# Threshold attention and a gated feed-forward part on one core: the kernel lays its own steps on the engines, and q, k and v come laid out for it

## The chip, the core and the metric

The kernel runs on one core of one Trainium2 chip. Five engines work there, each through its own instructions in order: PE (TensorE, matmuls and transposes into PSUM; its weight loads are listed as PEld), DVE (VectorE), ACT (ScalarE), POOL (GpSimd) and SP (SyncE, which here issues all DMAs). They wait for one another by semaphores. The metric is the device time of one execution in microseconds; lower is better.

## The reference

Eight batches, eight heads, 576 tokens, 64 channels a head. The first part is attention whose probabilities below a threshold are cut off; the second is a feed-forward part that mixes each token with the one before it.

```python
scores = scale * np.matmul(q, k.transpose(0, 1, 3, 2))
thresh = np.max(scores, axis=-1, keepdims=True) - tau
scores = np.where(scores >= thresh, scores, -1000000000.0)
attn = np.exp(scores - np.max(scores, axis=-1, keepdims=True))
attn = attn / (np.sum(attn, axis=-1, keepdims=True) + 1e-09)
x = np.matmul(attn, v)          # heads side by side: (8, 576, 512)
...
xk = mu_k * x + (1.0 - mu_k) * x_prev
xr = mu_r * x + (1.0 - mu_r) * x_prev
k = np.maximum(xk @ w_k, 0.0)   # w_k 512 x 1024
v = k * k @ w_v                 # w_v 1024 x 512
r = 1.0 / (1.0 + np.exp(-(xr @ w_r)))
return r * v
```

The weights come as float64 words, everything else as float32.

## The kernel before

**Precision.** Most products are made from split operands: a number is written as an upper part (a copy into a shorter float format, `fp32r`) and a lower part (what is left). A product then takes three matmuls, upper by upper, upper by lower and lower by upper. Making the two parts costs a copy on ACT and a subtraction on DVE or POOL.

**Attention.** A *job* is a batch and a pair of heads, 32 in all. Each has nine *query tiles* of 128 rows: four for each head, and one tile, called T, with the last 64 queries of both heads. A *slot* is a tile, 288 in all. In `prep_steps` a job's q and k are loaded as they lie, turned on PE (L189), copied and split by ACT, DVE and POOL into `hi` and `lo`, and `stack` copies these by DMA (L238 to L241) into stationaries `st` that hold a head's upper and lower part on top of each other, so that two matmuls of 128 rows do the three products. A tile then goes through `scores` (PE, L326), `row_max` (DVE, L338), `threshold` and `expo` (ACT, L342, L346), `mask` (DVE, L351), `denom` and `inverse` (DVE, L355, L358), `norm` (POOL, L361), `turn_p` (PE, five transposes, L368), `p_hi` (ACT, L393), `p_lo` (DVE, two instructions, L403), and, for a group of two tiles and a part of T, `attend` (PE, nine matmuls, L439) and `attend_out` (ACT L447, DVE L449 and L456), which writes x transposed into `xT` (first 512 tokens of a batch, two buffers) and `xE` (last 64).

The first jobs are made otherwise: job 0 multiplies scores in plain float32 (L308), and jobs 0 to 4 multiply probabilities by values in plain float32 (L412), which leaves out the split.

**Feed-forward part.** A *chunk* is 256 tokens; there are 18, two for each batch and two for the last 64 tokens of four batches each. `mix_steps` makes and splits xk and xr (POOL L485, L504, L510; ACT L497, L507). PE multiplies by w_k (tile h), w_r (z) and w_v (vps), all on L525; ACT takes the positive part (L551), DVE squares it (L554), ACT and POOL split it (L557, L558); the gate is on L586 and L590, its product with vps on DVE (L616), the store on L619. The weights are cut to float32 and split in 20 pieces by `weight_steps`, one every two slots from slot 4 on.

**Order.** The order is written by hand in `slot(n)`, which issues the steps of slot n together with those of the four tiles before it. Feed-forward matmuls are given out by a credit: a slot counts for 3.325 us of PE, what attention needs is taken off, and the rest is filled with steps of about 1.3 us; ten steps are kept in hand while chunks are still to come.

```python
TSLOT, TSTEP, KEEP, N0 = 3.325, 1.3, 10, 36
PLAIN, WHOLE = 5, 1
...
state["credit"] += TSLOT - tensor_time()
...
while state["credit"] > 0 and micro(keep):
    state["credit"] -= TSTEP
```

PSUM holds two buffers of scores, one of turned probabilities (`pt`) and two that all other products share. The first chunk can start when all four jobs of batch 0 are done, behind slot 36.

Of the kernel before, what the change touches and what calls it, by code (L numbers as in the profile page):

```python
# [8 lines left out]
F32 = mybir.dt.float32  # L9
# [6 lines left out]
# float32 readings of the upper words of the doubles 2**-127 and just under 2**128  # L16
W_MIN = 2.0 ** (0x38 * 2 - 127)
W_MAX = 2.0 ** (0x8F - 127) * (1 + 0x6FFFFF / 2.0**23)


@with_exitstack
def tile_threshold_attention_then_rwkv_ffn(
    ctx: ExitStack,
    tc: tile.TileContext,
    q: bass.AP,
    k: bass.AP,
    v: bass.AP,
    tau: bass.AP,
    mu_k: bass.AP,
    mu_r: bass.AP,  # L30
# [5 lines left out]
    nc = tc.nc  # L36
    V, A, G, PE, SY = nc.vector, nc.scalar, nc.gpsimd, nc.tensor, nc.sync

    B, H, S, D = q.shape
    DM, DF = w_k.shape  # L40
    P = 128
    NPAIR = H // 2
# [4 lines left out]
    NC4 = SM // P  # L47
    HS = S // 2
    KT = S
    KM = S + ST  # L50
# [4 lines left out]
    assert 2 * D == P and ST == D and NPAIR == NCT and B % NTB == 0  # L55
# [9 lines left out]
    wts = ctx.enter_context(tc.tile_pool(name="wts", bufs=1))  # L65
    p1 = ctx.enter_context(tc.tile_pool(name="p1", bufs=1))
    p2 = ctx.enter_context(tc.tile_pool(name="p2", bufs=2))
    p3 = ctx.enter_context(tc.tile_pool(name="p3", bufs=3))
    ps_s = ctx.enter_context(tc.tile_pool(name="ps_s", bufs=2, space=bass.MemoryType.PSUM))
    ps_t = ctx.enter_context(tc.tile_pool(name="ps_t", bufs=1, space=bass.MemoryType.PSUM))  # L70
    ps_w = ctx.enter_context(tc.tile_pool(name="ps_w", bufs=2, space=bass.MemoryType.PSUM))
    ctx.enter_context(tc.manual_schedule(engines={A.engine}))

    ident = const.tile([P, P], F32, name="ident")
    make_identity(nc, ident)
# [3 lines left out]
    tau_s = const.tile([P, 1], F32, name="tau_s")  # L79
    SY.dma_start(tau_s, tau.rearrange("(o t) -> o t", o=1).broadcast_to([P, 1]))  # L80
    ntau = const.tile([P, 1], F32, name="ntau")
    V.tensor_scalar(ntau, tau_s, 0.0, -1.0, op0=ALU.max, op1=ALU.mult)
    qscale = const.tile([P, 1], F32, name="qscale")
    V.tensor_scalar(qscale, tau_s, 0.0, 0.125, op0=ALU.is_ge, op1=ALU.mult)

    mu_sb = const.tile([P, 2, NCT], F32, name="mu_sb")
# [3 lines left out]
    xT = []  # L90
    for j in range(2):
        t = const.tile([P, NCT, SM + 1], F32, name=f"xT{j}")
        V.memset(t[:, :, 0:1], 0.0)
        xT.append(t)
    xE = const.tile([P, NCT, NE, ST + 1], F32, name="xE")

    vraw = const.tile([P, 2, 5 * D], F32, name="vraw")

    # stationaries of the scores' tile that holds both heads' last 64 queries
    bd = const.tile([P, 4, P], FR, name="bd")  # L100
    V.memset(bd.bitcast(F32), 0.0)

    # The weights come as float64 words.  Each is cut to float32 (saturating, with what
# [78 lines left out]
    def prep_steps(job):  # L182
# [48 lines left out]
        def stack(h):  # L231
            if job["whole"]:
                return
# [750 lines left out]
```

## Time and profile before

| | |
|---|---|
| Median of two runs | 1150.68 us (1149.67 to 1151.69) |
| Profiled execution | 1151.2 us from the first to the last instruction, 22514 instructions |
| Bytes moved by DMA | 105.61 MB in 125027 packets, 93681 of them under 512 B |
| Granted TensorE clock, mean | 0.995 |

The page's second part shows the span in 40 equal slices of 28.8 us; each digit is the busy share in tenths, 9 being 90% or more:

```profile
PE   6999989999999999989999999999999999999998
DVE  3899998888989898988989898989898989895222
ACT  3787877778687878768777878787878787876442
POOL 1465677465656465645747575656565656564672
DMA  5777334433344344433334444423344444300000
```

The first slices hold loading, weights and attention alone; the last three and a half hold the feed-forward part alone, in which only PE is full. A busy digit of PE says little by itself, because matmuls overlap one another and a row of waiting ones looks like a row of dense ones; the start times of neighbouring matmuls tell more. The chain of work that ended last goes over PE for 65% of the span, over DVE for 18% and over ACT for 10%.

### The profile page before, as it was taken

What the parts mean: (1) busy time and instruction counts of PE and PEld (TensorE: products, weight loads), DVE (VectorE), ACT (ScalarE), POOL (GpSimd) and SP (SyncE); (2) the same over time, 40 slices, a digit from 0 to 9 for tenths busy, and PEclk for the clock granted to TensorE, in tenths of its full rate; (3) what the DMA queues carried; (4) which work ended last, traced back from release to release, by engine and by line L of the source; (5) the groups of instructions that cost most, each with busy time, mean ns of one, the idle gap of its engine ahead of it and who ended that gap; (6) DMA issues with size and microseconds to landing.
All of it is one profiled execution on the core that took longest, in us unless ns stands there. A gap on an engine that the chain in (4) does not pass through costs nothing.

```text
span 1151.2 us, 22514 instructions
## 1 busy us (share of the span) xinstructions
PE 1104.4 (96%) x7454; PEld 999.1 (87%) x7454; DVE 961.3 (84%) x2399; ACT 846.0 (73%) x1775; POOL 673.3 (58%) x860
## 2 busy tenths in 40 slices
PE   6999989999999999989999999999999999999998
PEld 4887878898989898988989898989898989898997
DVE  3899998888989898988989898989898989895222
ACT  3787877778687878768777878787878787876442
POOL 1465677465656465645747575656565656564672
PEclk9999999999999999999999999999999999999999
DMA  5777334433344344433334444423344444300000
GB/s 131 184 205 204 83 85 93 113 85 74 70 95 105 84 112 95 112 88 71 83 83 104 92 104 104 99 68 87 79 102 94 104 98 99 76 29 13 25 20 18
DMA packets 125027, 105.61 MB, mean 92 GB/s; under 512 B 93681, under 2 KB 101873, under 8 KB 124913
## 3 DMA queue, kind: packets, MB, share of 16 engines
q1 hardware_dynamic: 124912, 104.18, 38.8%
q8 instruction: 60, 0.98, 0.3%
q14 instruction: 55, 0.44, 0.1%
HBM read 39.85 MB, written 9.44 MB: 43 GB/s over the span
## 4 chain that ended last, share of the span: by engine, by line
PE 65%; DVE 18%; ACT 10%; issue 4%; SPq 1%; DMA 1%; POOL 1%; DVEq 0%; ACTq 0%; POOLq 0%
PE h L525 12%; PE vps L525 12%; PE pt L368 10%; PE s L326 9%; PE o L439 9%; PE z L525 8%; DVE p L351 4%; DVE sm L338 3%; DVE plo L403 2%; ACT phi L393 2%; ACT p L346 2%; DVE r L554 2%; PE o L412 1%; DVE phi L403 1%; DVE xT L137 1%
## 5 line engine op out<-in xcount | busy, mean ns | idle before, releaser
L361 POOL TENSOR_SCALAR p<-p,sm 128x576 f32<-128x576 f32 x288 | 222.6, 773 | 255.2 <-DVE sm L358 187.4
L393 ACT ACTIVATE phi<-pt 128x640 fp32r<-128x640 f32 (+1 forms) x270 | 172.4, 649 | 111.3 <-PE pt L368 110.6
L351 DVE SCALAR_TENSOR_TENSOR p<-s,sm,p 128x576 f32<-128x576 f32 x288 | 233.7, 811 | 23.4 <-ACT p L346 19.1
L338 DVE TENSOR_REDUCE sm<-s 128x1 f32<-128x576 f32 x288 | 215.9, 750 | 21.2 <-PE s L308 10.3
L525 PE MATMUL h<-xk,wk 128*128 128x256 f32 x1728 | 231.8, 285 | 1.0 <-ACT r L551 0.3
L525 PE MATMUL vps<-wv,k 128*128 128x512 f32 x864 | 227.2, 399 | 2.0 <-DVE sg L616 1.8
L368 PE MATMUL pt<-ident,p 128*128 128x128 f32 x1440 | 210.4, 276 | 18.6 <-DVE phi L403 8.9
L525 PEld LDWEIGHTS h<-xk,wk 128*128 128x128 f32 x1728 | 216.0, 191 | 4.1 <-ACT r L551 2.1
L346 ACT ACTIVATE p<-s,sm 128x576 f32<-128x576 f32 x288 | 212.6, 738 | 1.4
L368 PEld LDWEIGHTS pt<-ident,p 128*128 128x128 f32 x1440 | 168.2, 142 | 45.9 <-issue 13.5
L403 DVE TENSOR_TENSOR plo<-pt,phi 128x512 fp32r<-128x512 f32 (+1 forms) x270 | 170.5, 632 | 39.6 <-ACT phi L393 33.7
L525 PEld LDWEIGHTS vps<-wv,k 128*128 128x128 f32 x864 | 154.2, 188 | 29.1 <-DVE sg L616 2.9
L439 PE MATMUL o<-phi,vs 128*128 128x256 f32 (+1 forms) x540 | 156.1, 312 | 2.5 <-ACT phi L393 1.6
L439 PE MATMUL o<-plo,vs 128*128 128x256 f32 (+1 forms) x432 | 118.7, 296 | 0.2 <-DVE plo L403 0.2
L326 PE MATMUL s<-st 128*128 128x288 f32 x496 | 112.1, 308 | 5.0 <-DVE p L351 4.2
L558 POOL TENSOR_TENSOR k<-r,k 128x512 fp32r<-128x512 f32 x72 | 93.2, 1295 | 35.6 <-ACT k L557 35.1
L525 PE MATMUL z<-wr,xr 128*128 128x512 f32 x432 | 112.8, 400 | 0.1
L326 PE MATMUL s<-st,st 128*128 128x288 f32 x496 | 107.4, 298 | 0.1
L439 PEld LDWEIGHTS o<-phi,vs 128*128 128x128 f32 x540 | 101.8, 189 | 5.3 <-ACT phi L393 3.3
L342 ACT ACTIVATE sm<-sm,ntau 128x1 f32<-128x1 f32 x288 | 84.5, 293 | 20.8 <-DVE sm L338 19.1
L554 DVE TENSOR_TENSOR r<-r 128x512 f32<-128x512 f32 x72 | 76.8, 1066 | 27.0 <-ACT r L551 26.5
L326 PEld LDWEIGHTS s<-st 128*128 128x128 f32 x496 | 81.8, 191 | 17.4 <-DVE p L351 9.5
(91 smaller groups left out, 1792.5 us busy)
## 6 DMA issues: line engine op xcount, KB each, us to landing
st<-hi SPq DMA_DIRECT2D x62, 288.0 KB, 3.3
st<-lo SPq DMA_DIRECT2D x62, 288.0 KB, 4.1
st<-hi SPq DMA_DIRECT2D x62, 144.0 KB, 3.9
st<-lo SPq DMA_DIRECT2D x62, 144.0 KB, 4.2
raw<-in_q SPq DMA_DIRECT2D x128, 64.0 KB, 2.5
raw<-in_k SPq DMA_DIRECT2D x64, 128.0 KB, 2.9
vraw<-in_v SPq DMA_DIRECT2D x32, 256.0 KB, 2.8
out<-sg SPq DMA_DIRECT2D x32, 256.0 KB, 2.4
```

Of the source, the lines that this page charges most:

```text
L326: PE.matmul(s[:, y, 0:HS], l, r[:, KT + y * HS : KT + (y + 1) * HS], start=(j == 0), stop=(j == n - 1),)
L338: V.tensor_reduce(x["sm"][0], x["s"], axis=AX.XY, op=ALU.max, negate=True)
L346: A.activation(x["p"].rearrange("p (a b) -> p a b", a=2), x["s"], AF.Exp, bias=x["sm"][0])
L351: V.scalar_tensor_tensor(pv, x["s"], thr, pv, op0=ALU.is_ge, op1=ALU.mult, accum_out=sums)
L361: G.tensor_scalar(x["p"], x["p"], x["sm"][3], 0.0, op0=ALU.mult, op1=ALU.add)
L368: PE.transpose(x["pt"][:, c, :], x["p"][:, o : o + P], ident)
L393: A.activation(hi[:, :, off : off + sl.stop - sl.start], x["pt"][:, :, sl], AF.Copy)
L403: V.tensor_tensor(d, x["pt"][0:n, y, sl], hi[0:n, y, cs].bitcast(F32), op=ALU.subtract)
L439: PE.matmul(o[:, 0:n], l, r, start=(j == 0), stop=(j == len(prods) - 1))
L525: PE.matmul(ps, l, r, start=(x == 0), stop=(x == len(prods) - 1))
L554: V.tensor_tensor(r, r, r, op=ALU.mult)
L558: G.tensor_tensor(k2[:, 1, js], r, k2[:, 0, js].bitcast(F32), op=ALU.subtract)
```

## The change

The kernel is written anew around a planner. Each step is recorded with its engine, the time it takes on it, its latency, what it reads and writes, and a priority; `Plan.order` goes through simulated time, always takes the step that can start earliest (by priority among equals), gives out the buffers as it goes, and `issue` then writes the instructions in that order. The planner's times are constants in the source. DMA issues are one more engine of the plan; they all go to SP.

```diff
+class Plan:
+    HOP = 0.05
+    def add(self, eng, occ, fn, reads=(), writes=(), key=0.0, lat=None, kb=0, wait=0.0):
+        ...
+    def order(self, loose=()):
+        ...
+        while len(out) < total:
+            best = None
+            for e, cand in open_.items():
+                ...
+                    t = max(t, f)
+                    k = (t, s.key, i)
+                    if pick is None or k < pick:
+                        pick = k
+                if pick is not None and (best is None or pick[0] < best[0]):
+                    best = (pick[0], e, pick[2])
+            ...
+            if e == "DMA":
+                pipe = max(pipe, t) + s.kb / 260.0
+                s.end = max(t + 2.2, pipe + 1.5)
+            else:
+                s.end = t + s.lat
```

Attention's matmuls have the priority of their slot less 1000, those of a chunk that of the slot that completes it less 30, so PE takes attention first whenever it is ready in the plan, and feed-forward steps of three matmuls otherwise. The pieces themselves change as follows.

- **Operands.** The host joins q and k, transposes them and puts two heads on the partitions; v, mu and the weights are laid out too. One load brings a job's q and k (L400, 576 KB), one its v. The transposes on PE are gone; ACT scales q (L404) and copies both to `hi` (L409), POOL makes `lo` (L415). The stacked copies (L436) stay.

```diff
-            SY.dma_start(
-                raw[:, 4:8, h], k[b, 2 * hp + h, 0:SM, :].rearrange("(p c) d -> p c d", c=NC4)
-            )
...
-                PE.transpose(ps[:, j * P : (j + 1) * P], raw[:, i].rearrange("p h d -> p (h d)"), ident)
...
+        raw = sbuf("raw", [P, W])
+        hi, lo = sbuf("hi", [P, W], FR), sbuf("lo", [P, W], FR)
+        add("DMA", 0.06, lambda: SY.dma_start(raw.get(), qk[b, hp]), writes=[raw], key=key - 9, kb=576)
...
+                "POOL",
+                1.41,
+                lambda cs=cs: G.tensor_tensor(
+                    lo.get()[:, cs], raw.get()[:, cs], hi.get()[:, cs].bitcast(F32), op=ALU.subtract
+                ),
...
+    qk = np.concatenate([q, k[:, :, m:], k[:, :, :m]], axis=2).transpose(0, 1, 3, 2).reshape(b, np_, 2 * d, -1)
```

- **No plain float32.** All jobs split scores and probabilities. The T tile takes its scores from `hi` and `lo` with three products in six matmuls instead of eight; its block stationaries `bd` have two buffers.

```diff
-            prods = [(bd[:, 2 * h + y], job["st"][h][0]) for h in range(2) for y in range(2)]
+            prods = [(bd, 0, None, hi), (bd, 0, None, lo), (bd, 1, None, hi)]
```

- **Pairs.** The sums of two slots are inverted together (L572, L573), and the two are then normalised and turned.

```diff
+        def invert():
+            V.tensor_scalar(sm.get()[:, 2], sm.get()[:, 2], 1e-9, None, op0=ALU.add)
+            V.reciprocal(sm.get()[:, 3], sm.get()[:, 2])
+        if o == 1:
+            add("DVE", 0.25, invert, ...)
...
+            turn(slots[n - 1])
+            turn(x)
```

- **Engines.** The square of the positive part goes from DVE to ACT (L830), a clamp of the weights from DVE to POOL (L346).

```diff
-                    V.tensor_tensor(r, r, r, op=ALU.mult)
+            add("ACT", 0.53, lambda r=r: A.activation(r.get(), r.get(), AF.Square), writes=[r], key=key - 1)
```

- **Batch 0 in halves.** Its four jobs become eight: first four tiles of every head pair, then the other five, so 36 jobs in all, and the operands of batch 0 are made twice. Its first chunk needs 16 slots instead of 36. The credit and the ten steps in hand are gone.

```diff
-TSLOT, TSTEP, KEEP, N0 = 3.325, 1.3, 10, 36
-PLAIN, WHOLE = 5, 1
+    HALF = 1
...
+        for part in range(2) if b < HALF else (None,):
+            for hp in range(NPAIR):
+                tiles = full if part is None else full[4 * part : 4 + 5 * part]
```

More of the change, by code (lines that the diff above doesn't have):

```diff
@@ L69, in tile_threshold_attention_then_rwkv_ffn @@
[L69 to L80, printed above, removed]
@@ new lines, in tile_threshold_attention_then_rwkv_ffn @@
+    ident = fixed("ident", [P, P])
+    add("POOL", 0.6, lambda: make_identity(nc, ident.get()), writes=[ident], key=-100)
+    small = fixed("small", [P, 4])
+    add(
+        "DMA",
+        0.06,
+        lambda: SY.dma_start(small.get()[:, 0:1], tau.rearrange("(o t) -> o t", o=1).broadcast_to([P, 1])),
+        writes=[(small, 0)],
+        key=-100,
+    )
+    add(
+        "DVE",
+        0.15,
+        lambda: V.tensor_scalar(small.get()[:, 1:2], small.get()[:, 0:1], 0.0, -1.0, op0=ALU.max, op1=ALU.mult),
+        reads=[(small, 0)],
+        writes=[(small, 1)],
+        key=-100,
+    )
@@ L353, in denom @@
[L353 to L368 removed]
+            st1, st2 = job["st"][h]
@@ new lines, in attend @@
+    def attend(job, h, g, key):
+        b, hp = job["b"], job["hp"]
+        n = 2 * P + (ST if job["tail"] and job["tg"] == g else 0)
+        hi, lo = job["groups"][h, g]
+        vs = job["vs"][h]
+        o = psum("w", [P, 512], 2)
+        prods = [(c, m) for c in range(4) for m in (hi, lo)] + [(4, hi)]
+        for j, (c, m) in enumerate(prods):
+            add(
+                "PE",
+                0.147 if n > 256 else 0.1195,
+                lambda j=j, c=c, m=m: PE.matmul(
+                    o.get()[:, 0:n], vs.get()[:, c], m.get()[:, c, 0:n], start=(j == 0), stop=(j == len(prods) - 1)
+                ),
+                reads=[vs, m],
+                writes=[o],
+                key=key - 1000,
+                lat=0.32,
+            )
@@ L517, in mix_steps @@
[L517 to L534 removed]
+                add("POOL", pool_tt, plus, reads=sr, writes=[d], key=key)
@@ L628, in ffn_chunk, with mm @@
-        order = "00 10 01 02 03 04 11 12 20 13 14 21 30 31 22 23 32 33"
-        mix = [parts[int(o[0])][int(o[1])] for o in order.split()]
-        return dict(micros=micros, mix=mix, first=kind == "main" and b0 == 0 and g == 0)
+            vps = psum("w", [P, DM], 2)
+            for ft in range(NFT):
+                w = pieces["v", ft, 0]
+                def mm(ft=ft, w=w, vps=vps, ts=ts):
+                    wt, x = w.get(), k2.get()
+                    prods = [(x[:, 0, ft, ts], wt[:, 0]), (x[:, 0, ft, ts], wt[:, 1]), (x[:, 1, ft, ts], wt[:, 0])]
+                    for i, (l, r) in enumerate(prods):
+                        PE.matmul(vps.get(), l, r, start=(ft == 0 and i == 0), stop=(ft == NFT - 1 and i == 2))
+                add("PE", 0.69, mm, reads=[w, *([k2] if ft == 0 else [(k2, (0, ft // 2)), (k2, (1, ft // 2))])], writes=[vps], key=key, lat=0.86)
@@ L937, in tile_threshold_attention_then_rwkv_ffn @@
-    for n in range(NS + 5):
-        slot(n)
-    while micro():
-        if state["gate"] is not None:
-            state["gate"]()
-            state["gate"] = None
-    flush_a()
-    while state["rest"] is not None:
-        flush_b()
-_INS = ["q", "k", "v", "tau", "moe_mu_k", "moe_mu_r", "moe_w_k", "moe_w_v", "moe_w_r"]
+        job["first"] = len(slots)
+        for t in job["tiles"]:
+            slots.append(dict(job=job, ji=ji, t=t, n=len(slots)))
+    wlist = [
+        (name, w, c, f)
+        for name, w in (("k", w_k), ("r", w_r), ("v", w_v))
+        for f in range(w.shape[1])
+        for c in range(w.shape[0])
+    ]
@@ L951 @@
+    plan.order(loose=("w", "r"))
+    plan.issue()
 def kernel(**inputs):
```

1408 lines of the change are left out of this document (702 added, 706 removed).

## The prediction

> **What bounds the kernel now.** I read the page's busy times first, then the busy times of three stages, then the rows of single engines in order of time. The page gives one execution of 1151.2 us, 0.05% over the median of the runs (1150.68), so sums made against it stand for both. The first stage ends where the first feed-forward matmul starts, the last begins where only feed-forward matmuls are left (columns: stretch, its length, busy us of PE, PEld, DVE, ACT, POOL, granted clock, DMA share, GB/s).
>
> ```profile
> span 1151.2 us, 22514 instructions
> PE 1104.4 (96%) x7454; PEld 999.1 (87%) x7454; DVE 961.3 (84%) x2399; ACT 846.0 (73%) x1775; POOL 673.3 (58%) x860
> ...
> 0.00:162.40 162.40, 141.41 (x901) 118.65 (x902) 134.38 (x318) 116.01 (x263) 84.07 (x115) 0.98 0.62 158
> 162.40:1050.00 887.60, 866.35 (x5984) 794.38 (x5983) 804.61 (x2054) 689.87 (x1441) 536.11 (x688) 1.00 0.39 88
> 1050.00:1151.20 101.20, 96.65 (x573) 86.04 (x571) 22.35 (x29) 40.08 (x73) 53.08 (x58) 1.00 0.07 21
> ...
> 162.44 1.60 PE L525 MATMUL h<-xk,wk 128*128 128x256 f32 x12
> ```
>
> In the middle PE is busy 97.6% and DVE 90.6%. Busy PE is not dense PE, so I take what a matmul costs from start to start in unbroken stretches (start, us, count).
>
> ```profile
> 501.12 0.43 PE L326 MATMUL s<-st 128*128 128x288 f32 x2
> 501.39 0.43 PE L326 MATMUL s<-st,st 128*128 128x288 f32 x2
> ...
> 502.64 0.30 PE L439 MATMUL o<-plo,vs 128*128 128x320 f32 x1
> 502.79 0.31 PE L439 MATMUL o<-phi,vs 128*128 128x320 f32 x1
> ...
> 508.15 0.74 PE L368 MATMUL pt<-ident,p 128*128 128x128 f32 x5
> 508.64 0.36 PE L439 MATMUL o<-phi,vs 128*128 128x256 f32 x1
> ...
> 508.96 0.28 PE L439 MATMUL o<-phi,vs 128*128 128x256 f32 x1
> 509.08 0.28 PE L439 MATMUL o<-plo,vs 128*128 128x256 f32 x1
> ...
> 158.98 1.47 PE L412 MATMUL o<-pf,vf 128*128 128x128 f32 x10
> ...
> 1063.07 11.51 PE h L525 x96
> 1074.58 5.47 PE z L525 x24
> 1080.05 10.88 PE vps L525 x48
> ...
> 1146.69 0.69 DVE L616 TENSOR_TENSOR sg<-vps,sg 128x512 f32<-128x512 f32 x1 [4.69 <-PE vps L525]
> ```
>
> So: two score matmuls 0.27 us; five transposes 0.49 (508.15 to 508.64), near 0.48 over many; an attention-times-values matmul 0.15 at 320 columns and 0.12 at 256; a tile in plain float32 1.47; a feed-forward chunk 11.51 + 5.47 + 10.88 = 27.86. In the order of before, 43 slots' transposes stand ahead of the first feed-forward matmul. Behind it stand 18 chunks (501.5), 245 slots of transposes (117.6), 1072 score matmuls (144.7), 230 transposes of q and k (22), 486 matmuls at 320 and 486 at 256 columns (131) and 24 plain tiles (35): 952 us of dense work between 162.4 and 1146.7, or 96.7%. Two losses remain: 3.3% there, and the start, in which PE does some 90 us of work in 162 (43 x 0.48, 58 x 0.096, 168 x 0.135, 21 x 1.47 and about 10 of float32 scores).
>
> **The change on PE.** It removes 288 transposes of q and k (27.6 us at 0.096) and 45 plain tiles (66 us), and gives those five jobs 20 groups of 9 matmuls (180 at 0.135, 24 us). The tail tile takes 6 score matmuls for 8 (31 x 0.27 = 8.4 us). The one float32 job of scores is not priced by a row here; its replacement is 38 matmuls, 5 us, and I bound the difference by 0 and 10. New total: 1216 score matmuls 164.2, 288 x 0.48 = 138.2, 576 x 0.15 + 576 x 0.12 = 155.5, 18 x 27.86 = 501.5, together 959. That is some 83 us less than 90 + 952, but much of it lay in the start, where PE was not full.
>
> **The first stage.** In PE's order before, the first feed-forward matmul stands behind 43 slots; here are the rows around it (pq turns q, s are scores, pt turned probabilities, o values, h feed-forward):
>
> ```order
> L368 MATMUL pt<-ident,p 128x128 x5
> L412 MATMUL o<-pf,vf 128x128 x5
> L189 MATMUL pq<-ident,raw 128x128 x4
> L326 MATMUL s<-st_0_1708 128x288 x2
> L326 MATMUL s<-st_0_1708,st_0_1709 128x288 x2
> L525 MATMUL h<-xk,wk_446 128x256 x3
> ```
>
> And on PE in the changed kernel (w is the shared accumulator, L821 the same feed-forward product):
>
> ```order
> L624 MATMUL pt<-ident,p 128x128 x5
> L507 MATMUL s<-st_878 128x288 x2
> L507 MATMUL s<-st_878,st_881 128x288 x2
> L624 MATMUL pt<-ident,p 128x128 x5
> L507 MATMUL s<-hi,bd_85 128x288 x2
> L507 MATMUL s<-lo,bd_85 128x288 x2
> L507 MATMUL s<-hi,bd_85 128x288 x2
> L821 MATMUL w<-xk,wk_134 128x256 x3
> ```
>
> It has moved ahead to slot 19, because batch 0 is cut in two halves. What must be done by then stands on DVE: 19 weight pieces, 20 maxima, 19 masks, 16 splits of turned probabilities, 9 inversions of a pair, 8 sums into xT. Their prices, from start to start on a full DVE, and for the weights from groups by shape:
>
> ```profile
> 502.72 0.76 DVE L338 TENSOR_REDUCE sm<-s 128x1 f32<-128x576 f32 x1
> 503.39 0.15 DVE L355 TENSOR_SCALAR sm<-sm 128x1 f32<-128x1 f32 x1
> 503.45 0.68 DVE L403 TENSOR_TENSOR plo<-pt,phi 128x512 fp32r<-128x512 f32 x1
> 504.05 0.16 DVE L358 RECIPROCAL sm<-sm 128x1 f32<-128x1 f32 x1
> 504.24 0.28 DVE L403 TENSOR_TENSOR phi<-pt,phi 64x128 fp32r<-64x128 f32 x1
> 504.55 0.43 DVE L449 TENSOR_TENSOR xT<-o,ot 64x256 f32<-64x256 f32 x1
> 504.90 0.22 DVE L456 TENSOR_TENSOR xE<-o,ot 64x64 f32<-64x64 f32 x1
> ...
> 505.46 0.82 DVE L351 SCALAR_TENSOR_TENSOR p<-s,sm,p 128x576 f32<-128x576 f32 x1 [0.34 <-ACT p L346]
> 506.20 0.75 DVE L338 TENSOR_REDUCE sm<-s 128x1 f32<-128x576 f32 x1
> ...
> L136 DVE TENSOR_SCALAR xT<-xT 128x512 uint32<-128x512 uint32 x20 | 12.8, 638 | 0.0
> L137 DVE SCALAR_TENSOR_TENSOR xT<-wk_words,xT 128x512 uint32<-128x512 uint32 x8 | 7.4, 928 | 0.0
> L138 DVE SCALAR_TENSOR_TENSOR xT<-wk_words,xT 128x512 uint32<-128x512 uint32 x8 | 6.3, 786 | 0.0
> ...
> wk_words<-in_moe_w_k SPq DMA_DIRECT2D x8, 512.0 KB, 6.1
> ```
>
> Maximum 0.67, mask 0.74, split 0.60 + 0.31, inversion 0.06 + 0.19, sum 0.35, a weight piece 2.35 (its clamp goes to POOL). That is 19 x 2.35 + 20 x 0.67 + 19 x 0.74 + 16 x 0.91 + 9 x 0.25 + 8 x 0.35 = 92 us. DVE cannot begin before a piece of weights has landed: the first stands on SP behind one job's load and four stacked copies, so it is issued between 2 us (nothing ahead waits) and 10 (load and ACT's two steps ahead of it); I take 7 as an estimate, 6.1 to land, and a step of ACT, so 14. At 95% cover 92 becomes 97, and the chain of differences, scaling and split behind the last sum is about 7. The stage ends near 118 us; 106 if DVE were dense and the chain overlapped, 136 if DVE were full only 80%. It holds 31 us of PE work.
>
> **The middle.** PE has 959 - 31 - 75 = 853 us there, but not evenly. Before, ten steps were kept in hand; in these rows of before, PE's order at slots 55 and 56, the value product vps runs between scores and transposes:
>
> ```order
> L525 MATMUL vps<-wv_1952,k_1937 128x512 x3
> L525 MATMUL vps<-wv_2063,k_1937 128x512 x3
> L326 MATMUL s<-st_0_2154,bd 128x288 x4
> L326 MATMUL s<-st_1_2213,bd 128x288 x4
> L439 MATMUL o<-phi,vs_2219 128x256
> L525 MATMUL vps<-wv_1434,k_1937 128x512 x2
> ```
>
> The changed order of PE has this at slots 58 to 60:
>
> ```order
> L507 MATMUL s<-st_2395 128x288 x2
> L507 MATMUL s<-st_2395,st_2398 128x288 x2
> L624 MATMUL pt<-ident,p 128x128 x5
> L507 MATMUL s<-st_2770 128x288 x2
> L507 MATMUL s<-st_2770,st_2774 128x288 x2
> L507 MATMUL s<-st_2770 128x288 x2
> L624 MATMUL pt<-ident,p 128x128 x5
> L507 MATMUL s<-st_2770,st_2774 128x288 x2
> L624 MATMUL pt<-ident,p 128x128 x5
> ```
>
> No feed-forward matmul is left to put there: the two chunks of batch 0 are used up at slot 52 and the next come with the end of batch 1. The same happens at slots 32 to 34, 95 to 100, 130 to 136, 239 to 244, 274 to 279 and two single ones, 37 slots in all. A slot of attention alone holds (38 x 0.135 + 9 x 0.48 + 18 x 0.27)/9 = 1.58 us of PE, but 0.67 + 0.74 + 0.125 + 0.93 + 0.20 = 2.67 of DVE, 2.8 at the same 95%. These 37 slots cost 104 us. The other 853 - 58 = 795 us of PE work I take at the density before, 96.7%: 822. DVE's relief (the squares go to ACT, the splits of q and k to POOL) should raise it, since DVE falls to about 2.67 us of every 3.3; a fixed order with less slack may lower it. Ends: 99% (803) and 92% (864).
>
> **What ACT, POOL and SP get.** Two rows price most of it:
>
> ```profile
> L557 ACT ACTIVATE k<-r 128x512 fp32r<-128x512 f32 x72 | 45.6, 633 | 16.9 <-DVE r L554 16.6
> L558 POOL TENSOR_TENSOR k<-r,k 128x512 fp32r<-128x512 f32 x72 | 93.2, 1295 | 35.6 <-ACT k L557 35.1
> ```
>
> ACT gets 72 squares, 72 x 0.63 = 45 us; scaling and copying a job's q and k in whole rows (36 x 3 x 0.7 = 76) takes the place of 62 large and 124 small copies (62 x 0.63 and 124 x about 0.25, 70). POOL gets 72 lower parts at 1.295 x 576/512 = 1.45, 104 us, and loses 62 small ones. Over a middle of 926 us that is 79% of ACT (690 + 45 of it) and about 67% of POOL: hidden by PE there, and if ACT's cover went, a chunk would show 4 x 0.63 = 2.5 us. SP's rows fall from 551 to 412.
>
> **The rest.** In PE's order 216, 72 and 144 feed-forward matmuls stand behind the last attention: 25.9 + 16.4 + 32.6 = 75 us, and from the end of the last product 4.5 us to the end, as before. Loads: fewer and larger packets, hidden from slot 19 on. Sum: 118 + 104 + 822 + 75 + 4.5 = 1124 us, 2.4% under the profiled 1151.2.
>
> **Rivals.** *The plan is dense* (0.20): start 106, 37 x 2.75, 803, 79.5: 1090 us. For it: DVE's slack; against it: before, no stage reached 99%.
>
> *Late stacks* (0.15, the slower side). One buffer each holds hi and lo, and the tail tile, five slots into a job, now reads them. The next job's hi, lo and stacked copies can start only behind its scores, four slots ahead of their first use.
>
> ```profile
> 507.00 0.56 SPq L238 DMA_DIRECT2D st<-hi  x1
> 507.66 0.53 SPq L239 DMA_DIRECT2D st<-lo  x1
> ...
> st<-lo SPq DMA_DIRECT2D x62, 288.0 KB, 4.1
> ```
>
> ACT about 1.2 (an estimate, twice a 512-column copy), POOL 2 x 1.45, three issues 1.6, landing 4.1, and 1.5 that I allow for waiting behind other work: 11.3 us against 4 x 3.3 = 13.2 in full slots, so free; in a bare slot, 4 x 2.8 = 11.2, just not. Were the chain some 4 us longer than that on the 31 boundaries, PE, in order, would stand for about 1.8 us each with all feed-forward work queued behind: 31 x 1.8 = 56, giving 1180 us. It decides from 1.6 us each.
>
> *A slow array* (0.15). After an idle stretch PE ran at half rate for a while:
>
> ```profile
> 31.98 0.77 PE L368 MATMUL pt<-ident,p 128*128 128x128 f32 x5
> ...
> 134.04 0.85 PE L326 MATMUL s<-st 128*128 128x288 f32 x2 [2.25 <-DVE p L351]
> 135.16 1.27 PE L368 MATMUL pt<-ident,p 128*128 128x128 f32 x5
> ```
>
> Five transposes took 1.27 us behind 2.25 idle, 0.77 otherwise. If the start and the 37 bare slots run so, PE's 1.58 becomes 3.16, more than DVE's 2.8: 37 x 0.4 = 13, and about 8 in the start: 1145 us. Against it: slots full at half rate are no longer idle. [...]
>
> **How the numbers follow.** The forecast holds 0.50, with its own range 1098 to 1150. The range for 8 in 10 reaches from below the dense plan to the edge of the late stacks: 1080 to 1175. This kernel's measurement can tell about 2% from no change: under 1127.7 is faster, over 1173.7 slower. Faster: 0.20 and 0.29 of the forecast's 0.50, 0.49. Slower: 0.13 and 0.02, 0.15. Within: 0.36.
>
> **What would show it.** First feed-forward matmul between 106 and 136 us; DVE at or over 90% busy until then; windows at slots 52 to 64 with PE busy well under DVE; a last stretch of 75 us with PE alone; score rows at each job's start with no wait on a stacked copy. I am wrong if scores wait on DMA or lower parts at most job starts, if the bare slots take over 3.3 us each, or if PE in full slots is under 92% dense.

## The result, and the profile after

The changed kernel takes 1252.99 us (1252.39 to 1253.58) for 1150.68: 1.089 times as long, 95% interval 1.086 to 1.092. The forecast was 1124, with a range of 1080 to 1175, so it has the direction wrong and the time lies outside the range. The profiled execution of the changed kernel spans 1250.6 us. First its page: span, busy times, the granted clock in 40 slices, and the shares of the chain that ended last.

```profile
span 1250.6 us, 20299 instructions
...
PE 1067.8 (85%) x6832; PEld 957.0 (77%) x6832; DVE 922.1 (74%) x2086; ACT 905.9 (72%) x1726; POOL 784.8 (63%) x902
...
PEclk9976698899899998999999999999999989999999
...
PE 42%; DVE 21%; ACT 14%; DMA 9%; issue 5%; POOL 5%; SPq 2%; POOLq 0%; ACTq 0%; DVEq 0%
```

PE and DVE are less full than before (they were at 96% and 84%), ACT is as full, POOL a little fuller (63% for 58%). The chain lies on PE for 42% where it was 65%, and on DMA for 9% where it was 1%: it runs to and fro between engines. Now the three stretches that the prediction used, cut at the first feed-forward matmul and behind the last matmul of attention (columns as there: stretch, length, busy us of PE, PEld, DVE, ACT, POOL, granted clock, DMA share, GB/s).

```profile
0.00:154.13 154.13, 61.87 (x263) 52.34 (x264) 111.37 (x197) 81.18 (x148) 121.81 (x104) 0.81 0.67 177
154.13:1170.80 1016.67, 930.75 (x6138) 838.33 (x6138) 806.03 (x1882) 789.86 (x1520) 627.38 (x753) 0.97 0.34 88
1170.80:1250.60 79.80, 75.19 (x434) 66.37 (x433) 4.72 (x8) 34.91 (x60) 35.60 (x46) 0.99 0.07 20
```

| | forecast | measured |
|---|---|---|
| start, to the first feed-forward matmul | 118 | 154.1 |
| middle, to the last matmul of attention | 926 (104 + 822) | 1016.7 |
| end (75 + 4.5) | 79.5 | 79.8 |

PE's work in the middle was forecast as 853 us of dense matmuls. Pricing every row of PE's timeline there with the same numbers (0.135 a score matmul, 0.096 a transpose, and so on) gives 854, so the amount of work is right; it fills 84% of the stretch. The other 163 us are gaps between starts that are longer than the price of what was started: 41 us of them stand between a product and transposes, 36 between scores and transposes. What ended PE's waits there (wait, us in total, times, longest):

```profile
PE pt L624 <- DVE phi L645: 34.4, 34, 2.5
PE s L507 <- DVE p L562: 10.1, 20, 2.4
PE pt L624 <- POOL p L589: 9.1, 14, 1.6
...
PE s L507 <- DMA st<-lo: 0.2, 1, 0.2
```

ACT's waits for the loads of q and k, in the same stretch:

```profile
ACT raw L404 <- DMA raw<-in_qk: 17.7, 13, 4.0
```

Listed waits are only part of the 163 us: PE is listed as idle for 86 us of the stretch (1016.67 less 930.75), and in the other 77 a matmul that started earlier is still listed as running. Both views name the same place: the turning of probabilities. PE waits for stacked copies only 0.2 us in the middle. ACT, though, waits 13 times for q and k.

To compare kernels that start feed-forward work at different times I use other marks: when the transposes of 36 and of 252 slots are done, and how much feed-forward work (168 matmuls a chunk, 27.86 us) was done by then. The transposes alone, changed kernel (columns: stretch, length, PE's busy us and instructions, PEld's, clock, DMA share, GB/s); 180 are 36 slots, 1080 are 216:

```profile
0.00:222.30 222.30, 34.81 (x180) 26.20 (x180) 0.85 0.62 161
222.30:1031.50 809.20, 159.97 (x1083) 124.11 (x1081) 0.97 0.35 89
```

By 222.3 us 156 feed-forward matmuls were done as well, 0.93 chunk or 26 us; between the marks 12.25 chunks. In the kernel before the marks stand at 136.1 us (no chunk) and 926.8 us (12.61 chunks between them).

One wait in the start is longer than any other of PE, the one for the first stacked copies, ahead of the first scores:

```profile
26.89 0.82 PE L507 MATMUL s<-st 128*128 128x288 f32 x2 [26.89 <-DMA st<-lo]
```

### The profile page after: what moved, and what is told of

Same layout as the page of the kernel before. It is cut to its first block, busy times and chain, and to the rows that moved or that the text cites. A ratio compares the mean times of both kernels' runs of the same rounds, so it can differ in the third digit from the quotient of the medians.

```text
span 1250.6 us, 20299 instructions
## 1 busy us (share of the span) xinstructions
PE 1067.8 (85%) x6832; PEld 957.0 (77%) x6832; DVE 922.1 (74%) x2086; ACT 905.9 (72%) x1726; POOL 784.8 (63%) x902
## 4 chain that ended last, share of the span: by engine, by line
PE 42%; DVE 21%; ACT 14%; DMA 9%; issue 5%; POOL 5%; SPq 2%; POOLq 0%; ACTq 0%; DVEq 0%
PE w L885 10%; PE w L821 9%; PE pt L624 7%; PE s L507 6%; PE w L667 6%; DVE p L562 5%; DVE plo L645 5%; DMA raw<-in_qk 5%; DVE sm L533 4%; PE w L863 4%; ACT phi L636 3%; DVE sm L572 2%; DVE phi L645 2%; SPq L436 2%; ACT p L554 2%
## 5 line engine op out<-in xcount | busy, mean ns | idle before, releaser
L821 PE MATMUL w<-xk,wk 128*128 128x256 f32 x1728 | 241.8, 288 | 0.3 <-DVE sg L891 0.3
L821 PEld LDWEIGHTS w<-xk,wk 128*128 128x128 f32 x1728 | 223.5, 192 | 0.8 <-DVE sg L891 0.5
L885 PE MATMUL w<-wv,k 128*128 128x512 f32 x864 | 213.8, 393 | 0.0
L667 PE MATMUL w<-phi,vs 128*128 128x320 f32 (+1 forms) x640 | 193.9, 324 | 5.9 <-ACT phi L636 5.9
L507 PE MATMUL s<-st 128*128 128x288 f32 x512 | 127.8, 333 | 70.8 <-issue 28.1
L885 PEld LDWEIGHTS w<-wv,k 128*128 128x128 f32 x864 | 157.4, 188 | 28.2
L667 PE MATMUL w<-plo,vs 128*128 128x320 f32 (+1 forms) x512 | 151.5, 316 | 7.2 <-DVE plo L645 7.0
L667 PEld LDWEIGHTS w<-phi,vs 128*128 128x128 f32 x640 | 130.0, 203 | 8.0 <-ACT phi L636 7.7
L415 POOL TENSOR_TENSOR lo<-raw,hi 128x576 fp32r<-128x576 f32 x72 | 102.7, 1439 | 47.0 <-ACT hi L409 45.0
L667 PEld LDWEIGHTS w<-plo,vs 128*128 128x128 f32 x512 | 104.4, 204 | 10.7 <-DVE plo L645 10.6
L863 PE MATMUL w<-wr,xk 128*128 128x512 f32 x432 | 112.2, 397 | 0.3 <-DVE xT L690 0.3
```

Of the source, the lines that this page charges most:

```text
L507: PE.matmul(s.get()[:, z, 0:HS], lt, r.get()[:, KT + z * HS : KT + (z + 1) * HS], start=(j == 0), stop=(j == len(prods) - 1),)
L667: lambda j=j, c=c, m=m: PE.matmul(o.get()[:, 0:n], vs.get()[:, c], m.get()[:, c, 0:n], start=(j == 0), stop=(j == len(prods) - 1)),
L821: PE.matmul(h.get()[:, f], l, r, start=(ct == 0 and i == 0), stop=(ct == NCT - 1 and i == 2))
L863: PE.matmul(z.get(), l, r, start=(ct == 0 and i == 0), stop=(ct == NCT - 1 and i == 2))
L885: PE.matmul(vps.get(), l, r, start=(ft == 0 and i == 0), stop=(ft == NFT - 1 and i == 2))
```

## The experiments

Unless said otherwise each is the changed kernel with one edit, timed beside the kernel before; ratios are to the kernel before, with 95% intervals. The changed kernel's own is 1.089.

### The planner's numbers and its pace

**The clamp on DVE.** The POOL clamp had turned out dear; this puts it back.

```diff
-            "POOL",
-            0.7,
-            lambda: G.tensor_scalar(t(), t(), W_MIN, W_MAX, op0=ALU.max, op1=ALU.min),
+            "DVE",
+            0.4,
+            lambda: V.tensor_scalar(t(), t(), W_MIN, W_MAX, op0=ALU.max, op1=ALU.min),
```

> Only the weights' clamp goes back from POOL (2.05 us each in the changed kernel) to DVE (0.47 us before). Theory that POOL's clamp is what stretches the start: 20 x 1.3 us of POOL and DVE's waits for it go, the first feed-forward matmul comes near 130 us instead of 154, and the whole near 1230 us. Rival, the start waits for DMA (stacked copies behind the weights): first feed-forward matmul still over 145 us, the whole within 8 us of 1253.

Measured: 1246.34 us, 1.081 [1.079, 1.083]; the first feed-forward matmul at 147.5. A gain of 7 us: real, but a small part. Both numbers are those of the rival, that the start waits for DMA: over 145 us, and within 8 us of 1253. The groups of the changed kernel and of this one (group, x count, busy us, mean ns, idle before):

```profile
L346 POOL TENSOR_SCALAR xT<-xT 128x512 f32<-128x512 f32 x20 | 40.9, 2054 | 8.1 <-ACT xT L338 8.0
```

```profile
L346 DVE TENSOR_SCALAR xT<-xT 128x512 f32<-128x512 f32 x20 | 14.8, 747 | 16.1 <-ACT xT L338 16.1
```

**Measured prices in the plan.** Times of the clamp, of weights' steps on DVE, of scaling, inversion, loads and DMA issues set to what the trace of the changed kernel shows.

```diff
-                pipe = max(pipe, t) + s.kb / 260.0
-                s.end = max(t + 2.2, pipe + 1.5)
+                pipe = max(pipe, t) + s.kb / 200.0
+                s.end = max(t + 2.6, pipe + 2.2)
...
-            0.7,
+            2.05,
...
-                0.25,
+                0.45,
```

> Same instructions, but the plan's constants are set to what the changed kernel's trace shows: clamp 2.05, weight steps on DVE 0.65, 1.0 and 0.9, scaling of q 0.7, inversion of a pair 0.45, a DMA issue 0.55, landing at least 2.6 us and 200 KB/us. Theory that the order is bad because the plan's times are wrong: the order fits the chip better, 1253 falls by 40 us or more, most of it in the start. Rival, the prices only matter at the margin: within 15 us of 1253.

Measured: 1257.23 us, 1.091 [1.089, 1.093]. So these constants are not the cause.

**Slack on every dependence.**

```diff
-    HOP = 0.05
+    HOP = 0.3
```

> Only the plan's allowance for a step from one engine to the next goes from 0.05 to 0.3 us, so an instruction stands behind its producer's by more other work. Theory that the in-order engines lack slack: PE's waits for a free pt (46 us of counted idle) and for scores shrink, full slots reach 94% dense, about 1200 us. Rival, slack was not the trouble and the plan only gets a longer chain: between 1245 and 1280 us.

Measured: 1343.25 us, 1.166 [1.164, 1.168]; from the 36th to the 252nd slot one comes every 4.15 us, for 3.75 in the changed kernel. The theory that the order only wants room falls in this form. That slack at every step lengthens loops that are already the limit is my reading; no run shows it.

**Feed-forward work spread out.** A feed-forward step may be planned only once a given slot has been turned, so that no bare slots are left.

```diff
+    for i, s in enumerate(ffn):
+        n = pace(i / 56)
+        if n is not None and n < len(slots):
+            s.deps.add(turned[n])
```

> Feed-forward matmuls may not run ahead of a pace (two chunks up to slot 72, then about two in 36 slots), so that none of the 37 bare slots is left; nothing else changes. Theory that bare slots and the half-rate array behind their gaps cost the middle: about 37 x (3.6 - 3.1) = 20 us by evenness and about 24 us of half-rate time, so near 1210 us, and a granted clock over 0.97. Rival, attention's own chain sets the pace at 3.7 us a slot however the rest lies: within 10 us of 1253, and slots take about as long as before.

Measured: 1252.9 us, 1.087 [1.085, 1.089]. The trace has 2 bare slots (no feed-forward matmul between one slot's transposes and the next) where the changed kernel has 38, and between the marks a slot comes every 3.72 us for 3.75. The bare slots, for which the prediction had a term of 104 us, are not what costs: without them a slot takes about as long.

### Pairs and buffers

**No pairs.** Each slot inverts, scales and turns by itself.

```diff
-        if o == 1:
+        if True:
...
-            turn(slots[n - 1])
             turn(x)
```

> Every slot inverts its own sum, is scaled and is turned by itself, as before the change, instead of two slots together; all else as changed. Pairing theory (the second mask of a pair holds back the first one's turning, and with 3 buffers of probabilities the next exponential): the pace of the middle falls from 3.77 us a slot (269 slots between the first feed-forward matmul and the last attention matmul of the changed kernel) to about 3.5, 70 us less, so 1180. Buffer theory (the loop through 3 buffers of probabilities is too short with or without pairs): at most 0.1 us a slot, 1225 to 1253. Disturbance theory (what the chip does besides the plan costs 0.2 us a slot whatever the order): within 1% of 1253.

**A control with one buffer of differences, and four buffers of probabilities.**

```diff
-            diff = sbuf("m", [P, 2, CH], F32, 2)
+            diff = sbuf("m", [P, 2, CH], F32, 1)
...
-        p = sbuf("p", [P, S], F32, 3)
+        p = sbuf("p", [P, S], F32, 4)
```

> Control for the next two: one buffer of feed-forward differences for two, which makes the room that a fourth buffer of probabilities needs; all else as changed. All theories: within 1% of 1253, since a chunk has 24 products of differences on POOL in some 60 us and few of them follow one another closely.

> Four buffers of probabilities for three (and one of differences, as in the control); pairs stay. Buffer theory: the exponential of a slot no longer waits for the turning of the slot three before it, and the second transposes of a pair no longer end a chain of 7 us: waits of the transposes on DVE's split and POOL's scaling fall from 43 us to under 20, the pace from 3.77 to 3.5, 1180. Pairing theory: the pair still waits for its second mask, but the next pair's first slot may run, half the gain, 1215. Disturbance theory: within 1% of the control.

**Both: four buffers and no pairs.**

> Four buffers of probabilities and no pairs (and one buffer of differences). Pairing and buffer theory together: pace 3.4 to 3.5, 1150 to 1180, no slower than the better of the two alone. If attention's loop is not the bound at all: within 1% of 1253.

Measured: no pairs 1222.66 us, 1.060 [1.058, 1.063]; control 1256.33, 1.089 [1.087, 1.092]; four buffers 1243.53, 1.079 [1.077, 1.081]; both 1231.98, 1.069 [1.067, 1.072]. Pairing costs 30 us, less than half of what its theory asked for. A fourth buffer is worth 13 us beside its control and nothing on top of single slots (where the control's edit is in it too). Neither is the main cause.

**Two inversions of one column.** Part of those 30 us could be something else that goes with pairs: the addition on two columns. The changed kernel's rows on DVE and POOL:

```profile
346.29 1.28 POOL L799 TENSOR_TENSOR xk<-m,xk 128x512 fp32r<-128x512 f32 x1
...
346.37 1.23 DVE L572 TENSOR_SCALAR sm<-sm 128x2 f32<-128x2 f32 x1
347.64 0.17 DVE L573 RECIPROCAL sm<-sm 128x2 f32<-128x2 f32 x1
```

This addition on 128 x 2 numbers lasts 1.23 us and ends with the POOL instruction that began just before it; the median of the 144 is 0.17. 33 of them lasted over 0.4 us and ended so; 36 others began while POOL was busy and lasted 0.37 us at most. The edit:

```diff
-            V.tensor_scalar(sm.get()[:, 2], sm.get()[:, 2], 1e-9, None, op0=ALU.add)
-            V.reciprocal(sm.get()[:, 3], sm.get()[:, 2])
+            for y in range(2):
+                c2, c3 = sm.get()[:, 2, y : y + 1], sm.get()[:, 3, y : y + 1]
+                V.tensor_scalar(c2, c2, 1e-9, None, op0=ALU.add)
+                V.reciprocal(c3, c2)
```

> Pairs stay, but each pair's sums are inverted in two times two instructions on one column instead of two on two columns. In the changed kernel about 35 of the 144 additions on two columns took 0.8 to 1.24 us and ended with a running POOL sum; on one column they took 0.15. If that hold carries the gain of the run without pairs: 1220 to 1235. If pairing itself carried it: 1245 to 1256.

Measured: 1246.40 us, 1.082 [1.079, 1.084]. The groups, changed kernel and this one:

```profile
L572 DVE TENSOR_SCALAR sm<-sm 128x2 f32<-128x2 f32 x144 | 53.0, 368 | 3.4
```

```profile
L574 DVE TENSOR_SCALAR sm<-sm 128x1 f32<-128x1 f32 x288 | 40.6, 141 | 1.0
```

The hold no longer shows (288 additions take 40.6 us where 144 took 53.0, and the mean is 141 ns for 368), and the edit was worth 7 of the 30 us. Why POOL held them was not shown: only 33 of the 69 additions that began while POOL was busy lasted over 0.4 us, and it was the form with two columns that was held. In the kernel before, 288 additions on one column took 132 to 156 ns each.

### The accumulator of turned tiles, the start, the clock

In the changed kernel the one buffer `pt` is held from the first transpose of a slot to the end of its split for 3.2 us of the 3.8 us to the next (means over 240 slots between 200 and 1100 us: 1.16 to ACT's copy, 0.97 to the split, 1.05 for the split). That suggested it as the limit.

**An accumulator that is released in parts.**

```diff
-        pt = psum("pt", [P, 5, P], 1)
+    turned_tile = plan.buf(ps, "pt", [P, 5, P], F32, make=lambda: ps.tile([P, 5, P], F32, name="pt"))
...
+        pt = turned_tile
```

> The turned tile's accumulator is one fixed tile in place of a pool's only buffer, so that the first four transposes of a slot wait for the split of the first four parts alone and not for that of the fifth, 0.28 us later; order and instructions are the same on every engine. Accumulator theory (one accumulator, held 3.2 us of a slot's 3.8 by transposes, ACT's copy and DVE's split, sets the pace): in 44% of the slots the transposes start within 0.25 us of the split's end, so 0.28 x 0.44 x 269 = 33 us less, 1220. If the accumulator doesn't set the pace: within 1% of 1253.

Measured: 1253.42 us, 1.088 [1.084, 1.091]. But this run's waits of PE show

```profile
PE pt L626 <- DVE phi L647: 48.3, 44, 3.8
```

that the transposes still wait for the split of the fifth part (it is the one that writes phi); the median time from its end to the next transposes is 0.29 us as in the changed kernel. The edit did not release anything earlier, so the run says nothing about the accumulator.

**Three mends at once, and later weights:** the clamp on DVE, no pairs, the fixed accumulator, and

```diff
-    W0, W1 = 6.0, 2.6
+    W0, W1 = 6.0, 5
```

> The changed kernel with the clamp on DVE, no pairs, the fixed accumulator, and the weights' pieces paced at 5 us instead of 2.6 behind the first. If the gains add (7 from the clamp, 30 from no pairs, 0 to 33 from the accumulator): 1183 to 1216. If an order that is laid this tightly holds PE up wherever it isn't mended: 1210 to 1225. Under 1150 only if the three are all there is.

Measured: 1208.58 us, 1.050 [1.047, 1.052], inside the range for gains that add and just under the other. Now the first feed-forward matmul stands at 114.0 us, where the prediction had 118. The marks: 36 slots at 206.0 us with 1.0 chunk, 252 slots at 992.2 us with 12.02 more. Moving the first feed-forward matmul 40 us forward moved the 36th slot only 16. It was no good mark for the end of the start.

**TensorE kept busy in the start.** In the changed kernel's start PE runs slowly: five transposes take nearly twice as long as the 0.74 us shown in the prediction.

```profile
34.70 1.33 PE L624 MATMUL pt<-ident,p 128*128 128x128 f32 x5 [1.49 <-POOL p L589]
```

The edit adds 172 products of the identity with itself, into a buffer that nobody reads; in the trace the last of them starts at 313.7 us.

```diff
+        fill = psum("w", [P, 512], 2)
+        add("PE", 0.29, lambda fill=fill: PE.matmul(fill.get()[:, 0:P], ident.get(), ident.get(), start=True, stop=True),
+            reads=[ident], writes=[fill], key=1e6, wait=12.0 + 0.8 * j)
```

> The changed kernel with some 170 matmuls of the identity with itself added on TensorE, 0.29 us each at full rate, spread over the first 150 us of its order, into a buffer that nobody reads. Half-clock theory (in the start five transposes take 1.3 us instead of 0.5, and they lie on a loop through the one accumulator of turned tiles): TensorE stays busy enough for its full rate, the first 36 slots are turned 20 to 30 us earlier, 1225 to 1235. If the start is bound elsewhere: 1253 to 1275, by the added work.

Measured: 1262.15 us, 1.096 [1.093, 1.098]. The transposes of the first 36 slots, to be read beside the row of the changed kernel above:

```profile
0.00:225.50 225.50, 28.93 (x180) 21.94 (x180) 0.89 0.62 160
```

They take 28.93 us for 34.81 at a granted clock of 0.89 for 0.85, so the filling did what it should; the 36th slot came no earlier (225.5 us with 1.0 chunk for 222.3 with 0.93). In the start the slow array is a companion of the idle time, not its cause. The middle was not filled.

### The other half alone

**The new layout under the old order.** The kernel before, with q, k, v laid out by the host, and otherwise its own order, plain jobs and credit. Only the time of a slot in the credit is set anew, 3.2 us for 3.325.

```diff
-    TSLOT, TSTEP, KEEP, N0 = 3.325, 1.3, 10, 36
+    TSLOT, TSTEP, KEEP, N0 = 3.2, 1.3, 10, 36
...
-            turn("pq", range(4))
...
+        SY.dma_start(raw, qk[b, hp])
...
+            A.activation(raw[:, 0:S], raw[:, 0:S], AF.Copy, scale=qscale)
...
+            A.activation(hi, raw[:, cols], AF.Copy)
+            G.tensor_tensor(lo, raw[:, cols], hi.bitcast(F32), op=ALU.subtract)
```

> The other half alone: the kernel before, its hand-written order, five plain jobs and float32 first job, with only q, k and v laid out by the host as in the change (no transposes of q and k, scaling and upper parts on ACT from whole rows, lower parts on POOL, natural order of tokens); its time of a slot in the order 3.2 us for 3.325, since a job has 9 transposes less. If the order of the change is what costs: PE, 97% dense in this order, has 288 x 0.096 = 27.6 us less to do, so 1123, range 1110 to 1140. If the layout costs (larger loads that land late, 104 us of lower parts on POOL): 1150 or more, up to 1250.

Measured: 1135.37 us, 0.985 [0.982, 0.988]: 1.5% faster than the kernel before. Its page and its marks:

```profile
span 1134.7 us, 21218 instructions
...
PE 1075.2 (95%) x7166; PEld 964.9 (85%) x7166; DVE 929.0 (82%) x2336; ACT 851.1 (75%) x1681; POOL 745.1 (66%) x860
```

```profile
0.00:130.00 130.00, 29.85 (x180) 21.33 (x180) 0.98 0.62 181
130.00:910.70 780.70, 156.66 (x1082) 122.49 (x1080) 0.99 0.37 92
```

So the layout, with its large loads and the lower parts on POOL, is no loss; with 3.325 us for a slot, as in the kernel before, it gains 0.6% (below). All of the loss, 118 us against this run, is in the rest: the order, the pairs, that no job is plain, batch 0 in halves with its operands made twice, the squares on ACT and the clamp on POOL, the other scores of T, the laid-out weights.

**The same, with one plain job for five.**

```diff
-    PLAIN, WHOLE = 5, 1
+    PLAIN, WHOLE = 1, 1
```

> The new layout under the old order, with only the first job plain where five were: 36 tiles are split for the two-part product, as the change does from its first slot on. If this arithmetic is what makes the change's start long: DVE gets 36 x 0.91 = 33 us more in a start that it fills to 83%, so 20 to 33 us more than the run of the new layout under the old order, 1155 to 1168. If the start of the change is long because of its order: 1130 to 1143.

Measured: 1169.99 us, 1.016 [1.014, 1.018], 35 us over the run before. Marks:

```profile
0.00:162.10 162.10, 35.62 (x180) 27.22 (x180) 0.81 0.50 143
162.10:943.50 781.40, 159.09 (x1082) 123.43 (x1080) 0.99 0.37 92
```

Of the 33 us between the two profiled spans (1167.4 and 1134.7) 32 lie ahead of the 36th slot (162.1 for 130.0): splitting 36 tiles more costs that much even in the old order, in a start in which PE had time for plain float32. Between the marks nothing changes (781.4 for 780.7, 12.65 chunks in both).

**Other paces in the old order.** Only the time of a slot, 3.2 us, is changed in the run with the new layout.

> The new layout under the old order, with 3.325 us for a slot in its order, the number of the kernel before, in place of 3.2: more feed-forward steps in each slot. If feed-forward work was paced too slowly (90 us of it behind the last attention at 3.2, where the kernel before has 80): 1125 to 1132. If it only shifts work: 1135, within 0.5%.

> As the last, with 3.45 us. If the pace of feed-forward work limits: 1118 to 1130. If the feed-forward backlog runs out and bare slots come up, or slots grow longer by what they take: 1135 to 1150.

> The new layout under the old order with 3.05 us for a slot in its order: fewer feed-forward steps in each slot. If a slot is as long as what the other engines get in it, feed-forward work included (8.5 us for each 0.125 in the three runs so far): 1122 to 1129. If work left over behind the last attention, where TensorE runs alone, weighs as much: 1133 to 1140.

> As the last, with 2.9 us: by the same line 1112 to 1120; if the work left over weighs as much, 1133 to 1145; under 1130 in either of the two would be faster by 2% than the kernel before.

Measured: 3.325 us 1143.57, 0.994 [0.993, 0.996]; 3.45 us 1153.00, 1.003 [1.001, 1.004]; 3.05 us 1143.58, 0.993 [0.991, 0.996]; 2.9 us 1156.40, 1.004 [1.003, 1.006]. In the last the feed-forward part falls so far behind that chunks mix tokens that a later batch has written over, so its time is that of the same work on other numbers. I had guessed wrong twice, first that more feed-forward steps would fill gaps, then that fewer would go on helping: 3.2 is the best of the five, and what lies on either side is that a slot gets longer, or that work is left behind the last attention.

## Why the prediction was wrong, point by point

**PE's work and the end: right.** The middle holds 854 us of work for 853 forecast, and the end takes 79.8 us for 79.5. "Hidden from slot 19 on" holds for PE's own waits, but not for ACT, which waits 17.7 us for q and k in the middle.

**The step that failed** is "the other 853 - 58 = 795 us of PE work I take at the density before, 96.7%: 822", together with the bare slots beside it. Measured, 38 bare slots take 3.30 us each, 125 us for 104, and the 794 us of work beside them take 891 us, a density of 89%: 21 and 69 of the 91 us that the middle is over. Two things are wrong in the step.

First, the 96.7% is a miscount. Behind the first feed-forward matmul stand 30 records of plain products, and a plain tile leaves ten: that is 3 tiles, 4.4 us, where the sum has 24 tiles and 35 us. The stretch then holds 921 us of work in 984, 93.6% (the middle alone 835 in 898, 93%), and the other 42 plain tiles lie in the start, where PE did about 121 us of work and not 90. With 93.6% the same sum gives 849 for 822, and 1151 us in all: no change. The bare slots happened to make up for a part: both terms together are 853 in 926, 92%.

Second, and this is the larger part: a density of the old order was carried over to a new one. Under the old order the new layout keeps 92% (815 of 890 us), and 91% with one plain job for five; the changed kernel keeps 84%, bare slots included. The sentence "a fixed order with less slack may lower it" had the right direction, but its lower end of 92% came from no row of an order like this one. That PE in full slots is under 92% dense was named as a sign of being wrong, and it is one that came; that the bare slots take over 3.3 us was another, and they stand just at it.

**The start was sized too small, and marked at the wrong place.** 154.1 us for 118. In the terms of its sum: DVE gets the first piece of weights at 21.5 us for 14, the last sum into xT ends 121.7 us later for 97, and the chain behind it takes 10.9 us for 7. DVE is busy 72% of the start, where 90% was the sign named. It is busy for 111 us where the sum has 92 us of work, priced from start to start; a piece of weights was priced at 2.35 us by the rows of w_k, and the 20 pieces take 55 us, 2.75 each. The clamp was left out of DVE's sum as if POOL gave it for nothing, while DVE's waits for it come to 23.7 us, the first piece's landing included; the run that moves it back gains 7.

```profile
L360 DVE TENSOR_SCALAR xT<-xT 128x512 uint32<-128x512 uint32 x20 | 14.2, 720 | 23.7 <-POOL xT L346 23.7
```

Giving up plain products was seen and priced as splits on DVE alone. For four of the five jobs it costs 35 us in the old order, nearly all ahead of the 36th slot; how much of it lies ahead of slot 19 was not measured.

**Where the 118 us against the best version lie**, by the marks, with feed-forward work taken at 27.86 us a chunk: 35 are the splits in place of plain products in four jobs (measured). The other 83, from 1167.4 to 1250.6 us of span, are spread: 34 ahead of the 36th slot (222.3 less 26 is 196, for 162), 39 up to the 252nd (809.2 for 781.4, and 0.40 chunk less done), 10 behind it. Of these 83 the edits made together take back 44: 30 by itself is what single slots bring, in which the held additions are 7, the clamp brings 7, and by subtraction, if gains add, 7 are left for the later weights. That leaves 39 us: by the same marks 16 ahead of the 36th slot (206.0 less 28 is 178, for 162) and 22 up to the 252nd (786.2 for 781.4, and 0.63 chunk less done).

**What is open: those 39 us.** In the start the trace names a candidate. The order without four of the plain jobs still makes the first job's scores in plain float32, from q and k as loaded, and PE's first scores start there at 7.82 us; in the changed kernel they wait for stacked copies until 26.89, and with the mends until 24.69.

```profile
7.82 4.21 PE L259 MATMUL s<-qk 64*128 64x288 f32 x8 [7.82 <-ACT qk L168]
```

No run gave the change that job back. For the middle there are several. The accumulator was not tested and is not ruled out: with one plain job under the old order it is held 3.0 us a slot, and slots come every 3.62 us between the marks; in the changed kernel 3.2 and 3.75. ACT waits for loads of q and k, 17.7 us in the changed kernel's middle, and in that run only for the first one. The squares stayed on ACT in every run of this order. And DVE's split waits four times as long for ACT's copy as in that run. Here are the changed kernel's wait, that with the mends and that run's, each between its first feed-forward matmul and its last matmul of attention:

```profile
DVE plo L645 <- ACT phi L636: 97.4, 109, 5.0
```

```profile
DVE plo L646 <- ACT phi L637: 56.1, 74, 3.1
```

```profile
DVE plo L354 <- ACT phi L344: 24.7, 46, 2.5
```

One such place, an extreme one, in the changed kernel's timeline (start, us, engine, line, operation, count, and in brackets the idle time before it and what ended it):

```profile
707.77 0.77 PE L624 MATMUL pt<-ident,p 128*128 128x128 f32 x5 [0.47 <-POOL p L589]
...
708.29 5.05 PE L885 MATMUL w<-wv,k 128*128 128x512 f32 x21
708.66 0.61 ACT L791 ACTIVATE xk<-m 128x512 fp32r<-128x512 f32 x1
...
709.66 1.04 POOL L768 TENSOR_TENSOR m<-xT 128x512 f32<-128x512 f32 x1
...
710.73 0.91 ACT L776 ACTIVATE mk<-m,mu_sb 128x256 f32<-128x256 f32 x2 [1.46 <-POOL m L768]
...
712.08 0.43 DVE L690 TENSOR_TENSOR xT<-w,r 64x256 f32<-64x256 f32 x1 [3.88 <-ACT r L681]
...
712.89 0.68 ACT L636 ACTIVATE phi<-pt 128x640 fp32r<-128x640 f32 x1
...
713.60 0.69 DVE L645 TENSOR_TENSOR plo<-pt,phi 128x512 fp32r<-128x512 f32 x1 [1.10 <-ACT phi L636]
...
715.23 0.71 PE L624 MATMUL pt<-ident,p 128*128 128x128 f32 x5
```

The turned tile is ready for ACT's copy at 708.54, but ahead of the copy ACT's order has a feed-forward scaling that waits 1.46 us for POOL, which comes to it late. The copy starts at 712.89, DVE has stood 3.88 us meanwhile, and the second tile of the pair is turned 7.5 us after the first. PE itself looks busy all the while with feed-forward work. A plan that starts each step as early as it can may put such feed-forward steps ahead of attention whenever they fit by its own clock. Over the whole middle, though, ACT's waits are a small part of this: from the end of the transposes to the copy pass 113.8 us in 269 slots, and in 102.9 of them ACT is busy with other steps; under the old order with one plain job it is 70.8 us in 248 slots. That this is where the 39 us go is a guess from one place; no run tested it.

**The rivals.** The dense plan is out: 84%. Late stacks are out in the middle, where PE waits 0.2 us for them; in the start the first ones are PE's longest wait, 26.9 us, which the rival did not mean. The slow array is there (granted clock 0.81 in the start and 0.97 in the middle), but the filled start shows that it decides nothing there; for the middle no run shows it. The half rate of its rows shows from start to start: five transposes took 1.06 us in the kernel before at 135.16 (to 136.22) and 0.49 at 508.15 (to 508.64). Idle time and a slow array come together in the changed kernel (PE is listed as busy for 62 of the start's 154 us at 0.81, and for 931 of the middle's 1017 at 0.97), and the clock of the first 36 slots went from 0.85 to 0.89 when PE was filled. The rival that should have stood in its place is plainer: an order that is laid to fit, run by engines that wait for one another in it, may be less dense than one in which each engine's steps stand a slot or two behind what they need. The runs agree with it, but none isolates it.

## What to carry to other kernels

Check what one record of a profile is before counting work by records: ten of them were one plain tile here. A density read from a profile belongs to the order that was profiled: carry over the amount of work, but price a new order by its own chain from one engine to the next and back, and not by the old share. Where a change brings a layout and an order, try each alone; here the layout is worth 1.5% with a slot's time set anew (0.6% without), and what else came with the new order costs 7% (1253 for 1170). And do not take away a spare engine's dear method in a stretch where that engine is idle: plain float32 on PE was the cheap one in the start, and splits in its place cost 35 us in four jobs.

## What the hardware showed unexpectedly

- The clamp to two bounds takes POOL 2054 ns on 128 x 512 numbers; DVE takes 747 in the run that puts it back (470 in the kernel before), and POOL's own scaling of 128 x 576 numbers takes 754.
- An addition on 128 x 2 numbers on DVE was held in 33 of 144 cases until a running POOL sum or difference ended, for 0.45 to 1.24 us in all where the median is 0.17; on 128 x 1 numbers the mean of 288 was 141 ns in the run with single columns, and the longest of 288 in the kernel before took 156.
- The granted clock doesn't tell all of it. The first 60 us of the changed kernel have it as full, the next 60 as 0.71 (columns as in the stretches above), yet five transposes take 1.33 us at 34.70 us already, in the row quoted for the start.

```profile
0.00:60.00 60.00, 16.32 (x63) 13.61 (x63) 32.82 (x58) 26.14 (x44) 38.21 (x34) 1.00 0.90 241
60.00:120.00 60.00, 25.67 (x108) 21.55 (x108) 48.53 (x80) 33.89 (x63) 56.91 (x44) 0.71 0.52 145
```
